# Attention and two expert layers on one core: the place of the turn of the maxima, of the last queries' transfers and of twelve remainders

## The chip, the cores and the metric

One core of one Trainium2 chip runs the whole program in one launch. The metric is the device time of that launch in microseconds (us), as the median of several runs. TensorE multiplies, VectorE, ScalarE and POOL (GpSimd) do the elementwise work, and SP issues nearly all DMAs; each of them works its own list of instructions strictly in order and waits for the others by semaphores.

## The reference

```python
# attention: batch 4, 8 heads, 576 positions, 64 per head
scores = (q @ k^T) / sqrt(64)
cum    = cumsum(log(clip(f, 1e-4, 1)))              # forget gates
scores = where(causal, -1e9, scores + cum[:, None] - cum[None, :])
scores = scores - max(scores)
attn   = exp(scores) / (sum(exp(scores)) + 1e-9)
x      = (attn @ v), heads side by side             # 2304 x 512
# first layer
h = ((x @ w1) * (x @ w2)) @ w3 ;  x = h @ w_out
# second layer: each row goes to the expert of its largest logit
e = argmax(x @ w_gate) ; out = gate(x) * sigmoid(x @ w_output_gate)[e] * (relu(x @ w1[e]) @ w2[e])
```

## The kernel before, in words

The attention runs over 16 pairs of heads (4 batches of 4 pairs). Each pair goes through the same stages, and pairs overlap: while one pair's probabilities are multiplied with its values, the next pair's scores are taken. The order of the work is written out by hand. `START` gives each stage of a pair a time in an imagined period of 9.8; `SHIFT` moves single stages of single pairs; all stages of all pairs are sorted by that time and issued in that order (L399 to L421), and every engine keeps that order. The numbers are places in a list, not times on the chip. `FILL` puts short products of zeros (L162) behind a stage, which only keep TensorE active.

The stages of pair n that matter here:

- `lk`, `lq`, `lv` load k, q and v (L188, SP). `kh`, `qh` round them to the short float format on ScalarE (L203), `kl`, `ql` take what is left over on VectorE (L210).
- `X1`, `X3`, `X2` are the scores by rows of queries (L217 by way of L219), each into a buffer of two PSUM banks; three such buffers go round. `m1`, `m3`, `m2`, `m0` take the row maxima on VectorE (L252).
- `qd` moves the last 64 queries of both heads into a block-diagonal tile `QD` by two DMAs (L205, L183). `XL` takes their scores (L244, L245), `mL` their maxima (L252).
- `Tm` turns the collected maxima by a product with the identity (L259), `tc` copies them out on ScalarE (L262), `mv` moves them by two DMAs into the row tile `MR` (L183).
- `GA` to `GD` are the scores once more, now by rows of keys and in full precision, and `HA` to `HD` add decay and maxima from `MR` to them in the same banks (L269); `eA` to `eD` take the exponentials on ScalarE (L289); `a0` to `a4` clear the part above the diagonal (L295) and `s1` to `s3` add the blocks up (L307), both on POOL.
- `p0`, `p1`, `p3` multiply the probabilities with the values (L316), `su` gives the sums (L332), both two pairs later in the list.
- For each batch, the sums are inverted: `rl` loads them, `rv` adds and takes reciprocals on VectorE (L356, L357), `rs` stores them (L359, SP). `xl` broadcasts the inverses for the first 512 rows (L74, SP) and `xm` multiplies them in on POOL (L367).
- `cr` clears, by one DMA of 771 KB in each of pairs 4 to 11, the rows `xs` into which the second layer's rows are scattered later (L377); the zeros are written on POOL (L375, L376).

Beside that, weights of the first layer are brought in as "pieces" of 512 KB each (class `Combined`, L424): step `c0` loads a piece (L462, SP), `c1` (ScalarE) to `c4` (VectorE) put its 64-bit numbers together as 32-bit ones (L469 to L475), `c5` rounds them on ScalarE (L478), and `c6` takes the remainder (L480), for the first 12 pieces on POOL, for all others on VectorE. One piece is done per pair. Behind the attention the pieces are multiplied, then both layers follow.

What stands in line in one period, before (phase in the period, from `START`):

```python
SP:      lq .3  ck 1.2  lk 2.6  zs 3.4  xl 4.2  rs 4.5  lv 5.7  c0 5.8  mv 6.6  rl 6.8  cr 7.6  qd 8.9
VectorE: kl 1.2  ql 1.3  c2 2.8  c3 3.4  c4 3.5  mL 3.5  m1 4.5  m3 7.3  m2 8.3  m0 8.6  rv 8.6
TensorE: GD, HD 1.5  XL 2.1  p0 3.3  Tm 3.6  X1 3.8  X3 4.7  X2 4.7  p1 5.1  p3 6.1  su 6.6  GA 8.4 ...
```

`X1`, `X3`, `X2` and `m1` to `m0` in this line belong to the next pair, `c3`, `c4` to an earlier piece.

Of the kernel before, what the change touches and what calls it, by code (L numbers as in the profile page):

```python
# [11 lines left out]
F32 = mybir.dt.float32  # L12
F32R = mybir.dt.float32r
# [15 lines left out]
P = 128  # L29
# [18 lines left out]

PERIOD = 9.8
START = {  # L50
# [8 lines left out]
}  # L59
SHIFT = {}  # L60

FILL = {(0, "X0"): 5, (0, "XL"): 10, (1, "X0"): 4, (1, "XL"): 4, (2, "X2"): 5, (2, "X0"): 5}

AFTER = {
    "K4_13": 4.4, "K4_14": 4.43, "K0_15": 15.6, "K0_16": 15.61, "K0_17": 15.62, "inputs": 11.36, "scores": 13.38,
# [11 lines left out]
def attention(nc, tc, ident, xT, rz, xs, wc, q, k, v, f):  # L77
# [7 lines left out]
    with (  # L85
# [16 lines left out]

        def decay_parts():
            SP.dma_start(out=fc, in_=f)
            V.tensor_scalar(out=fc, in0=fc, scalar1=1e-4, scalar2=1.0, op0=ALU.max, op1=ALU.min)
            A.activation(out=fc, in_=fc, func=ACTF.Ln)
            V.tensor_tensor_scan(c8, fc, fc, 0.0, ALU.add, ALU.bypass)
            V.tensor_scalar(out=EK[0:NH], in0=c8, scalar1=-8.0, scalar2=None, op0=ALU.mult)
            V.scalar_tensor_tensor(out=EK[NH:], in0=c8, scalar=-8.0, in1=EK[0:NH].bitcast(F32), op0=ALU.mult, op1=ALU.subtract)
# [15 lines left out]
        def rows(e, t):  # L125
            e.memset(t.bitcast(F32), 0.0)
            for h in range(2):
                e.memset(t[64 * h:64 * h + 3, :min(S, t.shape[1])].bitcast(F32), 1.0)

        def constants():  # L130
            rows(G, CKs[0])
            rows(V, OQ)
            for t in (OD, *QDs, *[t[:, S:] for x in KHs for t in x]):
                V.memset(t.bitcast(F32), 0.0)
            for h in range(2):
                V.memset(OD[64 * h:64 * h + 3, HALF[h]].bitcast(F32), 1.0)
                for t in (OQ, OD):
                    V.memset(t[64 * h:64 * h + 1].bitcast(F32), 0.0)
            V.memset(ones, 1.0)
            for t in Ms:  # L140
                V.memset(t, 0.0)
            G.memset(tri, 0.0)
            G.affine_select(
                out=tri[:, 512:640], in_=tri[:, 512:640], pattern=[[-1, P]],
                compare_op=ALU.is_ge, fill=NEG, base=0, channel_multiplier=1,
            )
            G.memset(tril, 0.0)
            for h in range(2):
                G.affine_select(
                    out=tril[64 * h:64 * h + 64, 512:S], in_=tril[64 * h:64 * h + 64, 512:S],  # L150
                    pattern=[[-1, SL]], compare_op=ALU.is_ge, fill=NEG, base=0, channel_multiplier=1,
                )
            for t in MRs + CKs[1:]:
                rows(G, t)
# [101 lines left out]
                )  # L256

        def turn(s):
            PE.matmul(s["x", 4][0:64, 896:1024], Ms[s["n"] % 2], ident, start=True, stop=True)  # L259

        def turned(s):
            A.activation(out=tl(s, "mt", (P,), F32R)[0:9], in_=s["x", 4][0:9, 896:1024], func=ACTF.Copy)  # L262

        def spread_maxima(s):
            t, MR = s["mt"], MRs[s["n"] % 2]
# [93 lines left out]
                    SP.dma_start(out=view(rz), in_=z)  # L359

        def first_tile(s, x):
            for i in {7: (0, 1), 11: (2, 3)}.get(s["n"], ()):
                d = tl(s, f"rb{i % 2}", (512,), bufs=1)
                if x == 0:
                    spread(nc, d, rz[i, :, 0:512])
                else:
                    G.tensor_tensor(out=xT[:, i, 0:512], in0=xT[:, i, 0:512], in1=d, op=ALU.mult)  # L367

        def clear_rows(s):

            e = s["n"] - 4
            if 0 <= e < E:
                if e == 0:
                    zt = st["zt"] = p3.tile([P, DM + 2], F32, name="zero", bufs=1)
                    G.memset(zt, 0.0)  # L375
                    G.memset(zt[:, DM + 1:], float(2 * N))  # L376
                SP.dma_start(out=xs[e * N:e * N + W].rearrange("(c p) d -> p c d", p=P), in_=st["zt"].unsqueeze(1).broadcast_to([P, W // P, DM + 2]))  # L377

        stages = {
# [44 lines left out]
class Combined:  # L424


    def __init__(self, nc, tc, xpool, raw, wo, w3t, last):
# [5 lines left out]
            self.pieces += [("o", j), (0, j), (1, j)]  # L433
            self.steps += [(0, j), (1, j)]
        self.at = {x: i for i, x in enumerate(self.pieces)}
        self.queue = [self.narrow(f"w{x}{j}", wo[j] if x == "o" else w3t[x, j], self.slot(i), None, nc.vector if i >= 12 else None) for i, (x, j) in enumerate(self.pieces)]
        self.done, self.acc, self.spare = [0] * 7, {}, None
        self.raw = [raw.tile([P, 8, 512], F32, name=f"raw{i}", tag="u") for i in range(2)]
        self.units = [None] * 3
# [853 lines left out]
```

## Time and profile before

| | |
|---|---|
| median of 3 runs | 795.99 us (795.97 to 798.34) |
| the profiled execution | 797.8 us, of it 796.2 us span from the first to the last instruction |
| TensorE busy | 772.3 us, 97% of the span |
| VectorE, ScalarE, POOL busy | 443.6, 276.3, 309.7 us |
| mean granted TensorE clock | 0.992 of full speed |

The profile lists, for one execution, the instructions of each engine with their start and length in us from the span's start. A line of the timeline gives start, length, engine, line of the kernel, operation, the tile written and the tiles read, their shapes, and in brackets how long the engine had idled before and what ended that. PEld is the loading of weights on TensorE, SPq the issuing of DMAs on SP: the length there is that of the issue, not of the transfer. A clock of 0.5 is 1.2 GHz, 1.0 is 2.4 GHz.

### The profile page before, as it was taken

The numbers are of one execution on the slowest core, as the hardware profiler recorded it, in microseconds if no ns is written. First come the engines' busy times: TensorE is split into PE (matmuls) and PEld (weight loads), VectorE is DVE, ScalarE is ACT, GpSimd is POOL, SyncE is SP. The second block draws the span as 40 slices with busy tenths as digits, with TensorE's granted clock in tenths as the row PEclk, the third lists the DMA queues.
The fourth block names the chain that finished last, engine by engine and source line by source line (L and its number), as shares of the span: only waits on it lengthen the run. The fifth ranks groups of instructions, "written<-read, shape, count | busy, mean of one in ns | idle before, by whom it ended". The sixth has DMA issues, their size and how long they took to land. (4 is left out here: it accounts for less than half of the span.)

```text
span 796.2 us, 13782 instructions
## 1 busy us (share of the span) xinstructions
PE 772.3 (97%) x5153; PEld 643.9 (81%) x5155; DVE 443.6 (56%) x986; ACT 276.3 (35%) x537; POOL 309.7 (39%) x343
## 2 busy tenths in 40 slices
PE   7999999899999999999999999999999999999995
PEld 4676776677888887887888788898797999999983
DVE  7687887887989723341341322346478735445620
ACT  2565666564566222212221221313321222322221
POOL 6577888994000210230230111033444444444520
PEclk9999999999999999999999999999999999999998
DMA  3556777425635110110100010053676556456460
GB/s 108 158 150 195 230 230 249 147 86 168 201 123 196 53 42 28 40 40 5 55 16 13 21 40 0 4 189 112 215 231 221 165 189 229 146 185 214 146 262 30
DMA packets 40212, 102.12 MB, mean 128 GB/s; under 512 B 8611, under 2 KB 9315, under 8 KB 39889
## 3 DMA queue, kind: packets, MB, share of 16 engines
q1 hardware_dynamic: 36960, 91.46, 35.9%
q0 software_dynamic: 3184, 9.77, 3.2%
q8 instruction: 41, 0.67, 0.4%
q14 instruction: 27, 0.21, 0.1%
HBM read 84.47 MB, written 16.51 MB: 127 GB/s over the span
## 5 line engine op out<-in xcount | busy, mean ns | idle before, releaser
L595 DVE TENSOR_TENSOR ga<-b,ga 128x512 f32<-128x512 f32 (+1 forms) x40 | 25.4, 636 | 144.0 <-PE b L567 143.2
L726 POOL DMA_INDIRECT xs<-xr,pos x18 | 19.5, 1084 | 173.5 <-DVE pos L720 126.6
L252 DVE CUSTOM_DVE_ANT_0 junk<-x,tri 128x256 f32<-128x256 f32 (+3 forms) x128 | 62.9, 491 | 24.3 <-PE x L217 16.5
L565 PE MATMUL h<-gh,ah 128*128 128x320 f32 (+4 forms) x224 | 67.2, 300 | 0.0
L566 PE MATMUL h<-gl,ah 128*128 128x320 f32 (+4 forms) x224 | 66.9, 299 | 0.0
L567 PE MATMUL h<-gh,al 128*128 128x320 f32 (+4 forms) x224 | 66.9, 299 | 0.0
L565 PE MATMUL b<-xh,w2h 128*128 128x512 f32 (+1 forms) x160 | 59.9, 375 | 0.0
L565 PE MATMUL a<-xh,w1h 128*128 128x512 f32 (+1 forms) x160 | 59.8, 374 | 0.0
L567 PE MATMUL a<-xh,w1l 128*128 128x512 f32 (+1 forms) x160 | 58.9, 368 | 0.0
L567 PE MATMUL b<-xh,w2l 128*128 128x512 f32 (+1 forms) x160 | 58.9, 368 | 0.0
L566 PE MATMUL a<-xl,w1h 128*128 128x512 f32 (+1 forms) x160 | 58.8, 368 | 0.0
L566 PE MATMUL b<-xl,w2h 128*128 128x512 f32 (+1 forms) x160 | 58.8, 368 | 0.0
L565 PE MATMUL y<-raw,gh 128*128 128x512 f32 x144 | 56.9, 395 | 0.0
L567 PE MATMUL y<-raw,gl 128*128 128x512 f32 x144 | 56.2, 390 | 0.0
L566 PE MATMUL y<-raw,gh 128*128 128x512 f32 x144 | 56.0, 389 | 0.0
L295 POOL TENSOR_SCALAR_AFFINE_SELECT PT<-PT 128x256 f32<-128x256 f32 (+1 forms) x80 | 42.3, 547 | 35.3 <-ACT PT L289 35.3
L597 ACT ACTIVATE gh<-ga 128x512 fp32r<-128x512 f32 (+1 forms) x40 | 23.6, 589 | 87.3 <-DVE ga L595 87.3
L558 POOL TENSOR_SCALAR bh<-rb 128x1024 fp32r<-128x1024 f32 x28 | 37.0, 1324 | 42.9 <-DMA rb<-e 41.0
L1019 DVE SCALAR_TENSOR_TENSOR hl<-h,hh 128x320 fp32r<-128x320 f32 (+4 forms) x56 | 25.3, 461 | 46.8 <-ACT hh L1018 46.6
L316 PE MATMUL v<-PT,vr 128*64 128x448 f32 (+4 forms) x384 | 50.8, 402 | 0.0
L581 POOL TENSOR_TENSOR xT<-xT,rz 128x512 f32<-128x512 f32 (+1 forms) x16 | 19.8, 1235 | 76.6 <-ACT w2h L478 76.5
L559 DVE TENSOR_TENSOR bl<-rb,bh 128x1024 fp32r<-128x1024 f32 x28 | 37.0, 1338 | 15.0 <-POOL bh L558 15.0
(613 smaller groups left out, 2116.2 us busy)
## 6 DMA issues: line engine op xcount, KB each, us to landing
ra<-e SPq DMA_DIRECT2D x28, 512.0 KB
rb<-e SPq DMA_DIRECT2D x28, 512.0 KB
w<-w3t SPq DMA_DIRECT2D x16, 512.0 KB
xs<-zero SPq DMA_DIRECT2D x8, 771.0 KB
vr<-v SPq DMA_DIRECT2D x16, 320.0 KB
kr<-k SPq DMA_DIRECT2D x16, 288.0 KB
qr<-q SPq DMA_DIRECT2D x16, 288.0 KB
wo<-wo SPq DMA_DIRECT2D x8, 512.0 KB
```

Of the source, the lines that this page charges most:

```text
L252: V.tensor_tensor_reduce(out=junk[:, :w], in0=s["x", i][:, 512 * h:512 * h + w] if i < 4 else s["x", i][:, 224:224 + S], in1=tri[:, 640 - ...
L295: G.affine_select(out=t, in_=t, pattern=[[0, 2], [1, w]], compare_op=ALU.is_ge, fill=0.0, base=0, channel_multiplier=-1,)
L316: PE.matmul(s["v"][HALF[h], 384 + q0:384 + q1], s["vr"][:, j, HALF[h]], place(s, j, h, q0, q1), start=(j == 0), stop=(j == 4 or q1 == P),)
L558: G.tensor_scalar(out=hi, in0=src, scalar1=1.0, scalar2=1.0, op0=ALU.mult, op1=ALU.mult)
L559: lo_eng.tensor_tensor(out=lo, in0=src, in1=hi.bitcast(F32), op=ALU.subtract)
L565: PE.matmul(ps, ah, bh, start=start and i == 0, stop=False)
L566: PE.matmul(ps, ah, bl, start=False, stop=False)
L567: PE.matmul(ps, al, bh, start=False, stop=stop and i == last)
L581: G.tensor_tensor(out=xv, in0=xv, in1=d, op=ALU.mult)
L595: V.tensor_tensor(out=ga[:, :w], in0=pb[:, :w], in1=ga[:, :w], op=ALU.mult)
L597: A.activation(out=gh[:, f, :w], in_=ga[:, :w], func=ACTF.Copy)
L1019: V.scalar_tensor_tensor(out=hl[:, f, :w], in0=ps[:, :w], scalar=0.0, in1=hh[:, f, :w].bitcast(F32), op0=ALU.max, op1=ALU.subtract)
```

## The change

The list is rearranged. The turn of a pair's maxima now stands behind the next pair's scores and writes into the free columns of the first of their buffers (not for the first and the last pair). The last queries' transfers come before the loads of values and piece and before the maxima's row, instead of behind the clearing. `c1` goes behind the copy of the turned maxima, `c6` one place before `mL`, and on VectorE for all pieces. The reciprocals `rv` go from behind `m0` to behind `mL`; the store `rs` stays where it is. The first 512 rows are multiplied one tile per pair (pairs 7, 8, 9, 10) instead of two in pair 7 and two in pair 11, and the zeros for the clearing are written in pair 2. In the first pair, `XL`, `mL` and what follows go ahead of the subtractions; some fills move. At the start, a part of the constants is written while the gates are loaded, and a one-column exponential behind the logarithm loads ScalarE's table early.

```diff
--- before.py
+++ after.py
@@ -48,18 +48,18 @@
 
 PERIOD = 9.8
 START = {
-    "lk": -16.99, "c0": -13.79, "c1": -10.39, "lq": -9.49, "ck": -8.57, "kh": -7.55, "c2": -7.02, "qh": -6.92,
-    "X1": -5.99, "m1": -5.27, "X3": -5.12, "X2": -5.07, "m3": -2.49, "X0": -1.58, "m2": -1.5, "m0": -1.24, "qd": -0.95,
-    "kl": 1.21, "XL": 2.1, "mL": 3.54, "Tm": 3.61, "tc": 3.98, "ql": 1.3, "mv": 6.59, "cr": 7.59, "GA": 8.35,
+    "lk": -16.99, "c0": -13.79, "c1": -4.9, "lq": -9.49, "ck": -8.57, "kh": -7.55, "c2": 2.78, "qh": -6.92,
+    "X1": -5.99, "m1": -5.27, "X3": -5.12, "X2": -5.07, "m3": -2.49, "X0": -1.58, "m2": -1.5, "m0": -1.24, "qd": -4.8,
+    "kl": 1.21, "XL": 2.1, "mL": 3.54, "Tm": 4.8, "tc": 4.85, "ql": 1.3, "mv": 6.59, "cr": 7.59, "GA": 8.35,
     "HA": 8.43, "GB": 8.46, "HB": 8.5, "GC": 8.77, "HC": 9.64, "eA": 10.17, "eB": 10.24, "eC": 11.25, "GD": 11.28,
     "HD": 11.31, "a0": 11.0, "a1": 11.6, "a4": 11.7, "c3": 13.19, "eD": 13.33, "c4": 13.3, "c5": 14.02, "lv": 15.51,
-    "s1": 13.9, "a2": 14.0, "a3": 14.1, "s2": 14.5, "c6": 17.0, "s3": 17.5, "p0": 22.91, "p1": 24.73,
-    "p3": 25.66, "su": 26.2, "xl": 33.6, "xa": 27.84, "sa": 28.24, "xm": 41.0, "zs": 32.77, "rl": 36.24, "rv": 57.6,
+    "s1": 13.9, "a2": 14.0, "a3": 14.1, "s2": 14.5, "c6": 23.12, "s3": 17.5, "p0": 22.91, "p1": 24.73,
+    "p3": 25.66, "su": 26.2, "xl": 33.6, "xa": 27.84, "sa": 28.24, "xm": 43.2, "zs": 32.77, "rl": 36.24, "rv": 62.36,
     "rs": 63.34,
 }
-SHIFT = {}
-
-FILL = {(0, "X0"): 5, (0, "XL"): 10, (1, "X0"): 4, (1, "XL"): 4, (2, "X2"): 5, (2, "X0"): 5}
+SHIFT = {(0, "XL"): -4.55, (0, "mL"): -5.9, (0, "Tm"): -1.8, (0, "tc"): -1.8, (0, "mv"): -3.49}
+
+FILL = {(0, "XL"): 10, (1, "X0"): 2, (0, "HA"): 3, (0, "HB"): 5, (1, "XL"): 4, (2, "X0"): 5, (1, "HA"): 2, (1, "HB"): 3}
 
 AFTER = {
     "K4_13": 4.4, "K4_14": 4.43, "K0_15": 15.6, "K0_16": 15.61, "K0_17": 15.62, "inputs": 11.36, "scores": 13.38,
@@ -102,8 +102,11 @@
 
         def decay_parts():
             SP.dma_start(out=fc, in_=f)
+            small_constants()
             V.tensor_scalar(out=fc, in0=fc, scalar1=1e-4, scalar2=1.0, op0=ALU.max, op1=ALU.min)
             A.activation(out=fc, in_=fc, func=ACTF.Ln)
+            A.activation(out=junk[:, 0:1], in_=Ms[0][:, 0:1], func=ACTF.Exp)
+            pads()
             V.tensor_tensor_scan(c8, fc, fc, 0.0, ALU.add, ALU.bypass)
             V.tensor_scalar(out=EK[0:NH], in0=c8, scalar1=-8.0, scalar2=None, op0=ALU.mult)
             V.scalar_tensor_tensor(out=EK[NH:], in0=c8, scalar=-8.0, in1=EK[0:NH].bitcast(F32), op0=ALU.mult, op1=ALU.subtract)
@@ -127,18 +130,24 @@
             for h in range(2):
                 e.memset(t[64 * h:64 * h + 3, :min(S, t.shape[1])].bitcast(F32), 1.0)
 
+        def small_constants():
+            rows(V, OQ)
+            for h in range(2):
+                V.memset(OQ[64 * h:64 * h + 1].bitcast(F32), 0.0)
+            for t in Ms:
+                V.memset(t, 0.0)
+
+        def pads():
+            for t in (*QDs, *[t[:, S:] for x in KHs for t in x]):
+                V.memset(t.bitcast(F32), 0.0)
+
         def constants():
             rows(G, CKs[0])
-            rows(V, OQ)
-            for t in (OD, *QDs, *[t[:, S:] for x in KHs for t in x]):
-                V.memset(t.bitcast(F32), 0.0)
+            V.memset(OD.bitcast(F32), 0.0)
             for h in range(2):
                 V.memset(OD[64 * h:64 * h + 3, HALF[h]].bitcast(F32), 1.0)
-                for t in (OQ, OD):
-                    V.memset(t[64 * h:64 * h + 1].bitcast(F32), 0.0)
+                V.memset(OD[64 * h:64 * h + 1].bitcast(F32), 0.0)
             V.memset(ones, 1.0)
-            for t in Ms:
-                V.memset(t, 0.0)
             G.memset(tri, 0.0)
             G.affine_select(
                 out=tri[:, 512:640], in_=tri[:, 512:640], pattern=[[-1, P]],
@@ -256,10 +265,12 @@
                 )
 
         def turn(s):
-            PE.matmul(s["x", 4][0:64, 896:1024], Ms[s["n"] % 2], ident, start=True, stop=True)
+            x = st[s["n"] + 1]["x", 1][:, 256:] if 0 < s["n"] < B * NP - 1 else s["x", 4][:, 896:]
+            s["t"] = x[0:64, :P]
+            PE.matmul(s["t"], Ms[s["n"] % 2], ident, start=True, stop=True)
 
         def turned(s):
-            A.activation(out=tl(s, "mt", (P,), F32R)[0:9], in_=s["x", 4][0:9, 896:1024], func=ACTF.Copy)
+            A.activation(out=tl(s, "mt", (P,), F32R)[0:9], in_=s["t"][0:9], func=ACTF.Copy)
 
         def spread_maxima(s):
             t, MR = s["mt"], MRs[s["n"] % 2]
@@ -359,7 +370,7 @@
                     SP.dma_start(out=view(rz), in_=z)
 
         def first_tile(s, x):
-            for i in {7: (0, 1), 11: (2, 3)}.get(s["n"], ()):
+            for i in {7: (0,), 8: (1,), 9: (2,), 10: (3,)}.get(s["n"], ()):
                 d = tl(s, f"rb{i % 2}", (512,), bufs=1)
                 if x == 0:
                     spread(nc, d, rz[i, :, 0:512])
@@ -369,11 +380,11 @@
         def clear_rows(s):
 
             e = s["n"] - 4
+            if e == -2:
+                zt = st["zt"] = p3.tile([P, DM + 2], F32, name="zero", bufs=1)
+                G.memset(zt, 0.0)
+                G.memset(zt[:, DM + 1:], float(2 * N))
             if 0 <= e < E:
-                if e == 0:
-                    zt = st["zt"] = p3.tile([P, DM + 2], F32, name="zero", bufs=1)
-                    G.memset(zt, 0.0)
-                    G.memset(zt[:, DM + 1:], float(2 * N))
                 SP.dma_start(out=xs[e * N:e * N + W].rearrange("(c p) d -> p c d", p=P), in_=st["zt"].unsqueeze(1).broadcast_to([P, W // P, DM + 2]))
 
         stages = {
@@ -433,7 +444,7 @@
             self.pieces += [("o", j), (0, j), (1, j)]
             self.steps += [(0, j), (1, j)]
         self.at = {x: i for i, x in enumerate(self.pieces)}
-        self.queue = [self.narrow(f"w{x}{j}", wo[j] if x == "o" else w3t[x, j], self.slot(i), None, nc.vector if i >= 12 else None) for i, (x, j) in enumerate(self.pieces)]
+        self.queue = [self.narrow(f"w{x}{j}", wo[j] if x == "o" else w3t[x, j], self.slot(i), None, nc.vector) for i, (x, j) in enumerate(self.pieces)]
         self.done, self.acc, self.spare = [0] * 7, {}, None
         self.raw = [raw.tile([P, 8, 512], F32, name=f"raw{i}", tag="u") for i in range(2)]
         self.units = [None] * 3
```

## Rows read from the trace of the kernel before

**Rows 1.** Windows: length; busy PE, PEld, DVE, ACT, POOL (instructions); clock, DMA share, GB/s.

```profile
10.00:190.00 180.00, 169.39 (x1802) 124.77 (x1801) 142.63 (x374) 101.36 (x171) 142.34 (x152) 0.98 0.57 178
190.00:510.00 320.00, 320.00 (x1482) 261.63 (x1481) 146.68 (x309) 99.05 (x189) 44.48 (x47) 1.00 0.18 58
```

**Rows 2.** Timeline of TensorE: the second turn and the last two.

```profile
28.00 0.43 PE L259 MATMUL xl<-ident,M 128*64 128x128 f32 x2
...
162.56 0.38 PE L259 MATMUL xl<-ident,M 128*64 128x128 f32 x2
...
172.19 0.27 PE L259 MATMUL xl<-ident,M 128*64 128x128 f32 x1
```

**Rows 3.** Timeline around the first clearing, and the window behind it.

```profile
62.83 0.41 SPq L377 DMA_DIRECT2D xs<-zero  x1
...
67.14 0.58 PE L244 MATMUL xl<-kh,QD 128*128 128x288 f32 x1 [1.90 <-DMA QD<-qh]
...
66.75:70.25 3.50, 3.11 (x12) 1.94 (x13) 0.77 (x2) 1.60 (x2) 2.34 (x3) 0.53 0.86 263
```

**Rows 4.** Timeline of the two pairs from 120 to 143 us.

```profile
120.14 0.43 PE L259 MATMUL xl<-ident,M 128*64 128x128 f32 x2
...
121.72 0.57 SPq L183 DMA_DIRECT2D MR<-mt  x1
...
126.29 0.40 PE L217 MATMUL gA<-MR,CK 64*128 64x288 f32 x2 [1.11 <-DMA MR<-mt]
...
129.91 2.53 POOL L367 TENSOR_TENSOR xT<-xT,rb 128x512 f32<-128x512 f32 x2
...
137.55 1.84 DVE L210 TENSOR_TENSOR ql<-qr,qh 128x576 fp32r<-128x576 f32 x1
...
142.89 0.43 PE L259 MATMUL xl<-ident,M 128*64 128x128 f32 x2 [1.93 <-DVE M L252]
```

**Rows 5.** Line 480, one remainder on POOL, one on VectorE: ns min/median/max, start.

```profile
L480 POOL TENSOR_TENSOR cw<-wo0u,cw x1: 1280/1280/1280, 51.0 to 51.0; 128x512 fp32r<-128x512 f32 x1
...
L480 DVE TENSOR_TENSOR gh<-wo4u,gh x1: 692/692/692, 190.7 to 190.7; 128x512 fp32r<-128x512 f32 x1
```

**Rows 6.** Timeline of an ordinary pair, from the queries' rounding to the row's use.

```profile
98.57 0.70 ACT L203 ACTIVATE qh<-qr 128x576 fp32r<-128x576 f32 x1
...
100.82 0.42 DVE L252 CUSTOM_DVE_ANT_0 junk<-x,tri 128x256 f32<-128x256 f32 x1 [0.99 <-PE x L217]
...
101.28 0.45 PE L217 MATMUL x<-CK,OQ 64*128 64x384 f32 x4
...
104.64 0.19 PEld L217 LDWEIGHTS gA<-MR,CK 64*128 64x128 f32 x2
```

**Rows 7.** Timeline of the start: first turn, third bank; and the window behind it.

```profile
16.44 0.43 PE L259 MATMUL xl<-ident,M 128*64 128x128 f32 x2 [1.79 <-DVE M L252]
...
22.30 0.60 PE L217 MATMUL gC<-qh,kh 64*128 64x448 f32 x4 [1.59 <-DVE M L252]
...
22.50:25.75 3.25, 3.25 (x26) 3.08 (x26) 1.67 (x3) 1.08 (x2) 0.06 (x1) 0.51 0.63 185
```

**Rows 8.** Timeline: a piece's issue and use, a row's issue and use.

```profile
15.45 0.42 SPq L462 DMA_DIRECT2D wo<-wo  x1
...
19.38 0.67 ACT L469 ACTIVATE wo0u<-wo 128x512 f32<-128x512 f32 x1 [2.20 <-DMA wo<-wo]
...
172.95 1.15 SPq L183 DMA_DIRECT2D MR<-mt  x2
...
175.45 0.29 PE L217 MATMUL gA<-MR,CK 64*128 64x288 f32 x2
```

**Rows 9.** Timeline: the reciprocals of a batch, and the store of one.

```profile
105.19 0.69 DVE L356 TENSOR_SCALAR z<-z 128x36 f32<-128x36 f32 x1
105.92 0.38 DVE L357 RECIPROCAL z<-z 128x36 f32<-128x36 f32 x1
...
151.00 0.65 SPq L359 DMA_DIRECT2D rz<-z  x1
```

## The prediction

> **What bounds the kernel now.** I read the windows first, then TensorE's timeline, then the queues. From 10 to 190 us, the attention, TensorE idles 10.6 us (180.00 - 169.39) at a mean granted clock of 0.98; in the 320 us behind it there is no idle time at all [rows 1]. So time won in attention arrives at the end undiminished, and it can only come from those 10.6 us and from the stretches at 1.2 GHz.
>
> The turn of the maxima (L259) marks a pair of heads. The last two stand 172.19 - 162.56 = 9.63 us apart with no wait on TensorE: that is its floor for a pair. From the second turn at 28.00 to the last at 172.19 there are 14 steps and 144.19 us, 9.4 more than 14 x 9.63 = 134.8 [rows 2]. I look for those 9.4, and for the start.
>
> **What is removed.**
> *Clearing.* In pair 4 SP's first clearing of `xs` leaves only at 62.83, because it waits for the memset of its zeros, which sits on POOL behind an addition and a remainder. The last queries' transfers are behind it on SP; TensorE idles 1.90 us for them at 67.14, and the clock then stands at 0.53 for the 3.5 us window: about 3.5 x 0.47 = 1.6 us more [rows 3]. The memset now runs two pairs earlier, with nobody on SP waiting (a short memset on POOL, whose slack hides it), and these transfers no longer stand behind a clearing. Gain 3.5; the lower bound is nothing, if another entry of SP's queue holds them.
>
> *First rows of the product.* From 120.14 to 142.89 two steps took 22.75, 3.5 over the floor. The four broadcasts of two tiles crowded the DMAs, so the maxima's row, issued at 121.72, kept TensorE waiting 1.11; then two multiplications on POOL (2.53 at 129.91) pushed its additions onto VectorE's subtractions (1.84 for one), and the turn waited 1.93 [rows 4]. Now one tile comes per pair, and POOL loses twelve remainders of 1.28 each [rows 5]. I take 3.0 of 3.5, since one multiplication still falls in each of four pairs; bounds 0 and 3.5.
>
> *The rest.* 9.4 - 3.5 - 3.5 = 2.4 us lie in small waits of the turn and in two pairs with reciprocals. Before the next scores, the turn waited for VectorE, and VectorE then idled 0.99 for the scores behind the turn [rows 6]. With the scores ahead, neither waits: 2.4, bounds 0 and 2.4.
>
> *Start.* TensorE waits 1.79 for the first turn and 1.59 before the third bank, and the clock is 0.51 for 3.25 us: 1.6 lost [rows 7]. The two subtractions leave the way to the first turn (nearest row 0.69 each [rows 5]), worth about 1.2; the fills moved behind the maxima's product keep TensorE active where it fell to 1.2 GHz, 1.6. In the second pair there is no probability product yet between turn and use of the row, so I give 1.0 back. Gain 1.8, bounds 0 and 3.4 (1.79 + 1.6). The early Exp table load and the split constants I cost at nothing: the warm-up matmuls cover them, and if that cover failed it would be one table load.
>
> **What is added.**
> *VectorE.* Twelve remainders at 0.69 [rows 5] stand ahead of the last queries' maxima. The cover is the 0.99 that VectorE now idles per pair [rows 6], so 0.3 remains: nothing. Upper bound 1.84 each, a subtraction of this kind when POOL is busy [rows 4]. On this pair of engines, the Trainium skill (SBUF — State Buffer, Who interferes with whom) says that a VectorE instruction with two SBUF inputs and a GpSimd instruction that reads SBUF block each other whole; by it a remainder could cost a whole POOL addition. That is the last rival below.
>
> *The row's way.* The last scores end at 101.28 + 0.45 = 101.73 with the turn (0.43 [rows 4]) ahead of them; with the turn behind, they end and it starts at 101.3. From the turn's start to the row's issue it is 172.95 - 172.19 = 0.76 [rows 2, 8], so the row leaves at about 102.1. Its first use loads weights at 104.64 [rows 6]: 2.55 us later. On an idle queue that does: in the last pair the row issued at 172.95 is in use at 175.45 without a wait [rows 8]. But the last queries' transfers now stand ahead of `v` and the piece, and SP must wait for `qh`, done at 98.57 + 0.70 = 99.27 [rows 6]. Two issues like the row's (1.15) and one of `v`, taken as long as a piece's (0.42) [rows 8]: the piece leaves at about 100.9, just ahead of the row. A piece took 19.38 - 15.45 = 3.93 us to its use behind another load [rows 8], here to 104.8; a row behind it is late by about 0.15. Ten loaded pairs: +1.5. Bounds: 0 (the row overtakes) and 2.0 each, as the crowded row took 126.29 - 121.72 = 4.57 [rows 4]. The idle-queue row alone would put this term at 0. The Trainium skill (DMA: Bandwidth & Descriptors, Queues, rings and completion order) says that each DMA engine takes descriptors in ring order; by that the row does wait for the load before it, which is the side I took.
>
> *The reciprocals.* They move from behind the scores' maxima to just behind the last queries' maxima, and their store on SP (`rs`) keeps its place, now ahead of the last queries' transfers. Before, SP found them done. Now, in the frame of rows 6, that maximum ends at about 99.8 (0.99 before 100.82), the reciprocals last 106.30 - 105.19 = 1.1 [rows 9], so the store leaves at 100.9 and takes 0.65 [rows 9], the queries' two 1.15, `v` 0.42: the piece at 103.2, the row at 103.6. Queued behind the waiting store are all of these, and TensorE waits for the row. It lands at 103.6 + 2.5 = 106.1 on an idle queue, 103.2 + 3.93 = 107.1 with the piece; used at 104.64. So 1.5 to 2.5 late; I take 2.4, as the piece is always there. It happens in two pairs (the third store comes after the last pair): +4.8.
>
> **Sum.** -3.5 - 3.0 - 2.4 - 1.8 + 1.5 + 4.8 = -4.4. The profiled execution took 797.8 around its span of 796.2, 1.8 above the median of the runs, 795.99; the difference taken off the median gives 791.6.
>
> **Rivals.**
> 1. *The store doesn't bite* and the row keeps up: VectorE runs ahead in those pairs, or the small row overtakes. For it: even in the crowded pair the row was only 1.11 late [rows 4]. Against: SP works strictly in order. 791.6 - 4.8 - 1.5 = 785.3.
> 2. *The clock falls after both stores.* TensorE idles 2.4 us there; 1.90 and 1.59 were followed by 1.2 GHz [rows 3, 7], 1.93 at 142.89 was not. Each fall costs 1.6: 794.8.
> 3. *Slower: the row is late in every loaded pair.* Place: the maxima's product of the first bank, on the DMAs behind `v`, the piece and the clearing. With 1.0 us in ten pairs for 0.15: +8.5, 800.1. It decides from (4.4 + 1.5) / 10 = 0.6 us per pair on. For it: 4.57 in the crowded pair; against: that pair also had four broadcasts.
> 4. *VectorE becomes the bound*: remainders of 1.84, 0.85 over the cover, twelve times: +10.2, 801.8. Against: POOL has 1.28 less to do per pair, right where the subtractions were slowed.
>
> **Numbers.** Forecast 0.36, rival 1 0.27, rival 2 0.22, rival 3 0.10, rival 4 0.05. This kernel can tell about 0.3% (2.4 us) from no change: faster is below 793.6, slower above 798.4. The forecast's own range is 788.5 to 794.5. Faster: most of the forecast (0.33), rival 1 (0.27), a third of rival 2 (0.07): 0.67. Slower: rivals 3 and 4 less a part that ends within: 0.12. Same: 0.21. The range leaves out what is slowest: 784.5 to 797.5.
>
> **What would show it.** Right: no wait for the last queries' transfers at the fifth pair and no clock below 1 there; turns mostly 9.6 to 9.9 apart; in two pairs a wait of TensorE for the row (L183) of about 2.4 us, with the reciprocals' store on SP directly before the queries' transfers; idle time of VectorE before the next scores' maxima gone; the first turn near 15.2. Wrong: waits for the row in every pair (rival 3), TensorE waiting for maxima in most pairs (rival 4), or no wait at all in the reciprocals' pairs (rival 1).

## The result, and the profile after

The changed kernel takes 808.07 us (median of 4 runs, 807.56 to 808.88) against 796.05 for the kernel before beside it: ratio 1.0145, 95% interval 1.0124 to 1.0165, so 11.5 us slower. The forecast was 791.6, with a range of 784.5 to 797.5: wrong in sign and outside its range. The profiled execution has a span of 805.9 us, 9.7 more than before.

The windows of the changed kernel, with the columns of [rows 1]:

```profile
10.00:190.00 180.00, 166.09 (x1717) 125.31 (x1715) 137.65 (x378) 100.13 (x164) 112.07 (x135) 0.97 0.53 168
10.00:15.00 5.00, 4.25 (x22) 2.51 (x19) 4.17 (x15) 1.37 (x2) 3.55 (x6) 0.66 0.35 98
66.75:70.25 3.50, 3.46 (x31) 2.17 (x32) 2.41 (x8) 2.48 (x4) 3.50 (x5) 1.00 0.16 53
90.00:95.00 5.00, 3.75 (x25) 2.76 (x27) 3.13 (x11) 2.94 (x5) 3.80 (x5) 0.80 0.40 120
165.00:170.00 5.00, 3.31 (x34) 3.21 (x36) 2.05 (x4) 1.89 (x3) 0.41 (x1) 0.81 0.34 115
170.00:175.00 5.00, 4.96 (x44) 3.57 (x44) 1.82 (x7) 3.01 (x5) 4.61 (x6) 0.85 0.12 20
190.00:510.00 320.00, 320.00 (x1501) 259.74 (x1498) 150.80 (x315) 99.05 (x187) 49.86 (x53) 1.00 0.20 64
```

TensorE now idles 13.9 us of the attention's 180 instead of 10.6. At the fifth pair, where [rows 3] had a clock of 0.53, it is 1.00. The clock falls in three other places: ahead of the first turn, between 10 and 15 us, where it stood at 1.00 before; near 93; and near 168 us. Each fall costs about 1.7 us, as (1 - 0.66) x 5 for the first. The 320 us behind the attention are full, as before. So the loss lies in the attention.

The timeline of the changed kernel at some of the turns (now L270):

```profile
28.48 0.43 PE L270 MATMUL x<-ident,M 128*64 128x128 f32 x2
...
39.95 0.32 PE L270 MATMUL x<-ident,M 128*64 128x128 f32 x1
...
49.97 0.13 PEld L270 LDWEIGHTS x<-ident,M 128*64 128x64 f32 x1 [0.17 <-DVE M L261]
49.97 0.32 PE L270 MATMUL x<-ident,M 128*64 128x128 f32 x1
...
53.40 0.18 PEld L226 LDWEIGHTS gA<-MR,CK 64*128 64x128 f32 x2 [0.19 <-DMA MR<-mt]
...
128.34 0.32 PE L270 MATMUL x<-ident,M 128*64 128x128 f32 x1
...
174.72 0.32 PE L270 MATMUL x<-ident,M 128*64 128x128 f32 x1
182.80 0.27 PE L270 MATMUL xl<-ident,M 128*64 128x128 f32 x1
```

From 28.48 to the last at 182.80 are 14 steps as in [rows 2], 154.32 us, 10.1 more than there. A plain one (39.95 to 49.97) takes 10.02, where the floor of [rows 2] is 9.63: the loading of the weights waits 0.19 for the row, and 0.17 for a maximum at the turn. Most of the rest lies in three stretches: the four steps from 70.07 to 115.48 (pairs 6 to 9), of 11.2 to 11.7 each, and the two pairs with reciprocals, 12.86 (115.48 to 128.34) and 14.95 (159.77 to 174.72). The first step, 28.48 to 39.95, takes 11.47; it belongs to the start.

The first reciprocals' pair, SP's queue and TensorE:

```profile
112.40 1.86 DVE L367 TENSOR_SCALAR z<-z 128x36 f32<-128x36 f32 x1
114.30 0.38 DVE L368 RECIPROCAL z<-z 128x36 f32<-128x36 f32 x1
114.70 0.63 SPq L370 DMA_DIRECT2D rz<-z  x1
115.44 0.52 SPq L192 DMA_DIRECT2D QD<-qh  x1
...
115.48 0.32 PE L270 MATMUL x<-ident,M 128*64 128x128 f32 x1 [1.04 <-DVE M L261]
...
116.69 0.54 SPq L197 DMA_DIRECT2D vr<-v  x1
117.29 0.42 SPq L473 DMA_DIRECT2D w<-w3t  x1
117.80 1.20 SPq L192 DMA_DIRECT2D MR<-mt  x2
...
120.91 0.40 PE L226 MATMUL gA<-MR,CK 64*128 64x288 f32 x2 [1.95 <-DMA MR<-mt]
```

And the second:

```profile
158.99 0.67 SPq L370 DMA_DIRECT2D rz<-z  x1
...
159.77 0.32 PE L270 MATMUL x<-ident,M 128*64 128x128 f32 x1 [0.77 <-DVE M L261]
...
162.72 1.21 SPq L192 DMA_DIRECT2D MR<-mt  x2
...
166.69 0.40 PE L226 MATMUL gA<-MR,CK 64*128 64x288 f32 x2 [3.45 <-DMA MR<-mt]
```

Store, queries' transfers, `v`, piece and row stand in the order that the forecast gave, and TensorE waits for the row: 1.95 and 3.45. The turn, too, waits 1.04 and 0.77 for maxima that now stand behind the reciprocals on VectorE; the first of these waits makes the step to 115.48 long. Behind the second wait for the row the clock stands at 0.81 and 0.85 for 10 us, worth (0.19 + 0.15) x 5 = 1.7.

Pairs 6 to 8 show something the forecast did not have. First the kernel before, SP's queue behind a row, then the changed one:

```profile
80.71 1.14 SPq L183 DMA_DIRECT2D MR<-mt  x2
...
82.63 0.46 SPq L377 DMA_DIRECT2D xs<-zero  x1
83.13 1.92 SPq L183 DMA_DIRECT2D QD<-qh  x2
...
85.10 0.59 SPq L188 DMA_DIRECT2D qr<-q  x1
...
89.02 0.68 ACT L203 ACTIVATE qh<-qr 128x576 fp32r<-128x576 f32 x1 [0.48 <-DMA qr<-q]
...
90.49 0.39 PE L217 MATMUL x<-kh,qh 64*128 64x256 f32 x2
```

```profile
82.05 1.18 SPq L192 DMA_DIRECT2D MR<-mt  x2
...
84.01 0.45 SPq L388 DMA_DIRECT2D xs<-zero  x1
84.52 1.98 SPq L197 DMA_DIRECT2D qr<-q  x1
...
90.10 0.68 ACT L212 ACTIVATE qh<-qr 128x576 fp32r<-128x576 f32 x1 [1.81 <-DMA qr<-q]
...
90.83 0.39 PE L226 MATMUL x<-kh,qh 64*128 64x256 f32 x2 [1.25 <-ACT qh L212]
```

Behind the clearing stood the transfers of the last queries; now the load of the *next pair's* queries stands there. In this pair its issue is held for 1.98, the data land 5.6 behind its start (90.10 - 84.52), where they took 3.9 before (89.02 - 85.10), and the scores wait 1.25 for them; the clock then stands at 0.80 and 0.86 from 90 to 100, another 1.7. At 79 and 126 us the scores wait 0.44 and 0.31 for rounded queries.

### The profile page after: what moved, and what is told of

Its sections match the earlier page's. It is cut to its first block, busy times and chain, and to the rows that moved or that the text cites. A ratio compares the mean times of both kernels' runs of the same rounds, so it can differ in the third digit from the quotient of the medians.

```text
span 805.9 us, 13785 instructions
## 1 busy us (share of the span) xinstructions
PE 778.5 (97%) x5156; PEld 650.7 (81%) x5156; DVE 443.5 (55%) x998; ACT 279.4 (35%) x538; POOL 285.1 (35%) x331
## 5 line engine op out<-in xcount | busy, mean ns | idle before, releaser
L261 DVE CUSTOM_DVE_ANT_0 junk<-x,tri 128x256 f32<-128x256 f32 (+3 forms) x128 | 62.8, 490 | 22.0 <-PE x L226 13.6
L306 POOL TENSOR_SCALAR_AFFINE_SELECT PT<-PT 128x256 f32<-128x256 f32 (+1 forms) x80 | 34.7, 454 | 66.5 <-ACT PT L300 64.2
L327 PE MATMUL v<-PT,vr 128*64 128x448 f32 (+4 forms) x384 | 54.1, 404 | 0.0
L570 DVE TENSOR_TENSOR bl<-rb,bh 128x1024 fp32r<-128x1024 f32 x28 | 36.4, 1315 | 15.3 <-POOL bh L569 15.3
```

Source lines behind the costliest of these rows:

```text
L261: V.tensor_tensor_reduce(out=junk[:, :w], in0=s["x", i][:, 512 * h:512 * h + w] if i < 4 else s["x", i][:, 224:224 + S], in1=tri[:, 640 - ...
L306: G.affine_select(out=t, in_=t, pattern=[[0, 2], [1, w]], compare_op=ALU.is_ge, fill=0.0, base=0, channel_multiplier=-1,)
L327: PE.matmul(s["v"][HALF[h], 384 + q0:384 + q1], s["vr"][:, j, HALF[h]], place(s, j, h, q0, q1), start=(j == 0), stop=(j == 4 or q1 == P),)
L570: lo_eng.tensor_tensor(out=lo, in0=src, in1=hi.bitcast(F32), op=ALU.subtract)
```

## The experiments

The kernel before ran beside each of them, with medians from 796.05 to 798.78, so the ratios are compared and not the medians; "us" in the table is (ratio - 1) x 796. By the medians alone three of the differences from the change that follow come out smaller: 10.9 for recip_back, 4.9 for clear_later and 9.1 for store_later, instead of 12.3, 6.9 and 10.3. The edits are to the changed kernel unless said otherwise, and show only the entries that differ.

| kernel | median us | ratio (95%) | against before, us |
|---|---|---|---|
| the change | 808.07 | 1.0145 (1.0124 to 1.0165) | +11.5 |
| recip_back | 797.21 | 0.9991 (0.9973 to 1.0009) | -0.7 |
| clear_later | 803.15 | 1.0058 (1.0034 to 1.0082) | +4.6 |
| row_first | 810.54 | 1.0181 (1.0112 to 1.0250) | +14.4 |
| turn_back | 813.73 | 1.0190 (1.0148 to 1.0232) | +15.1 |
| recip_clear | 794.53 | 0.9953 (0.9936 to 0.9969) | -3.7 |
| recip_qd | 801.92 | 1.0038 (1.0021 to 1.0056) | +3.0 |
| recip_clear_pool | 795.19 | 0.9959 (0.9947 to 0.9972) | -3.3 |
| zeros_early | 794.26 | 0.9948 (0.9931 to 0.9964) | -4.1 |
| zeros_tiles | 792.78 | 0.9932 (0.9909 to 0.9954) | -5.4 |
| zeros_tiles_rem | 793.81 | 0.9942 (0.9921 to 0.9964) | -4.6 |
| start_added | 795.26 | 0.9963 (0.9949 to 0.9977) | -2.9 |
| start_clear | 794.84 | 0.9961 (0.9943 to 0.9979) | -3.1 |
| store_later | 798.99 | 1.0016 (0.9997 to 1.0035) | +1.3 |
| store_clear | 795.95 | 0.9971 (0.9954 to 0.9987) | -2.3 |

### One part of the change undone

**recip_back**: the reciprocals go back behind the next scores' maxima.

```diff
-"rv": 62.36
+"rv": 57.6
```

> The change with one number taken back: the reciprocals stand behind the scores' maxima again, so SP finds them done. Theory (SP's queue: the store waits for the reciprocals, and the row of maxima, values and piece wait behind the store): the two waits of TensorE for the row in the reciprocals' pairs (1.95 and 3.45 us) and the clock's fall behind the second (about 1.7) go, about 7 us less than the change's 808.1: 801. Rival (VectorE's load is the loss, wherever its work stands): within 1 us of 808.1.

One due time is worth 12.3 us (1.0145 - 0.9991), more than the theory's 7, and with it the kernel stands level with the one before.

**clear_later**: the clearing goes behind the next queries' load.

```diff
-"cr": 7.59
+"cr": 11.2
```

> The change with the clearing issued behind the next queries' load instead of ahead of it. Theory (SP's queue: the later turn lets the row, and with it the clearing and the next queries' load behind it, leave later, so the rounded queries are late for the scores, which now stand ahead of the turn): the waits of the scores for the rounded queries in pairs 6 to 10 go, with the clock's fall in pair 8: about 4 us less than 808.1, 804. Rival (VectorE's load): within 1 us of 808.1, since nothing on VectorE changes.

6.9 us (1.0145 - 1.0058), more than the 4 expected, and the rival is out. The turns of pairs 4 to 8 are 9.75 to 10.05 apart, and behind 30 us no scores wait for rounded queries; the reciprocals' pairs still take 11.99 and 14.84.

**row_first**: the row goes ahead of `v` and the piece.

```diff
-"lv": 15.51, "c0": -13.79
+"lv": 16.45, "c0": -13.1
```

> The change with the loads of values and piece issued behind the row of maxima instead of ahead of it. Theory (the row waits for transfers issued just ahead of it): the 0.2 us per loaded pair, the 1.1 us of pair 1 and part of the waits in the reciprocals' pairs go: about 4 us less than 808.1, 804. Rival (the row is late only because the turn is later): less than 1 us.

A miss: no gain. Its timeline:

```profile
81.57 1.17 SPq L192 DMA_DIRECT2D MR<-mt  x2
82.83 0.34 SPq L197 DMA_DIRECT2D vr<-v  x1
...
84.46 1.97 SPq L197 DMA_DIRECT2D qr<-q  x1
...
90.36 0.39 PE L226 MATMUL x<-kh,qh 64*128 64x256 f32 x2 [1.36 <-ACT qh L212]
```

In plain pairs the row comes to its product in time (two steps of 9.71 between the turns at 38.29 and 57.71), but `v` now stands between row and load too, and the scores wait for queries in seven pairs, 0.6 to 1.5 each. What one stage wins on this queue, the next one pays.

**turn_back**: the turn ahead of the next scores again, in its own buffer.

```diff
-"Tm": 4.8, "tc": 4.85
+"Tm": 3.61, "tc": 3.98
-x = st[s["n"] + 1]["x", 1][:, 256:] if 0 < s["n"] < B * NP - 1 else s["x", 4][:, 896:]
+x = s["x", 4][:, 896:]
```

> The change with the turn alone put back ahead of the next scores, into the last queries' own buffer; everything else as changed. Theory (the turn's place starts both chains on SP): the row leaves 1.45 us earlier, the rounded queries are needed 0.4 us later, about 5 us less than 808.1: 803, with the waits behind the reciprocals' store left. Rival (the turn's move is a gain, as the prediction had it, and the loss comes from the other parts): 808 to 812.

A miss too. (The edit also moves the first pair's turn ahead.) The row does not leave earlier against the scores, since the queries' transfers, `v` and the piece are still ahead of it on SP; it is late by 0.7 to 1.4 in several pairs, and by 3.29 and 3.43 in the two with the store. With the early queries' transfers and the early store, the turn's place is not what costs.

### Two causes, or one

**recip_clear**: `rv` and `cr` both back.

> The changed kernel with two due times put back: the reciprocals behind the next scores' maxima (rv 57.6) and the clearing behind the queries' load (cr 11.2). Theory (two separate losses on SP's queue: the store that waits for the reciprocals, worth 808.1 - 797.2 = 10.9, and the queries' load behind row and clearing, worth 808.1 - 803.2 = 4.9, which add): 808.1 - 10.9 - 4.9 = 792.3, no wait of the scores for rounded queries left, steps of 9.7 to 10.1 in pairs 4 to 9. Rival (one loss that either edit relieves, an overfull SP queue): about 797, no better than the reciprocals alone.

0.9953 of 796.05 is 792.3: the theory's number, but in part by luck, since the theory added differences of medians. By the ratios the two edits alone give 12.3 and 6.9, and together 15.3 (1.0145 - 0.9953): two losses, but they overlap by some 4 us. From 80 to 120 us TensorE is without a gap but for 0.04, and the step from 90.43 to 100.39 is 9.96. What is left is elsewhere; the worst place of its timeline:

```profile
148.80 1.74 POOL L378 TENSOR_TENSOR xT<-xT,rb 128x512 f32<-128x512 f32 x1
...
149.32 1.77 DVE L491 TENSOR_TENSOR raw<-w11u,raw 128x512 fp32r<-128x512 f32 x1
...
151.02 0.75 DVE L261 CUSTOM_DVE_ANT_0 junk<-xl,tril 128x576 f32<-128x576 f32 x1
...
151.83 0.51 PE L226 MATMUL x<-kh,qh 64*128 64x384 f32 x4 [1.47 <-DVE M L261]
```

A remainder on VectorE that starts during POOL's multiplication takes 1.77; the others of this kind take 0.68 to 0.89 in this trace. The rest of the multiplication (150.54 - 149.32 = 1.22) and 0.69 make 1.91. The maxima behind it come late and TensorE waits 1.47. This happened in one of the four pairs with a multiplication. The Trainium skill (SBUF — State Buffer, Who interferes with whom) says that an instruction of VectorE with two SBUF inputs contends with one of GpSimd that reads SBUF, and that this contention is an exclusive lock; this row agrees with it, nearly to the sum.

**store_later**: only the store moves, behind the row; VectorE's order is the changed kernel's.

```diff
-"rs": 63.34
+"rs": 66.0
```

> The changed kernel with the reciprocals' store moved behind the maxima's row on SP (rs 66.0); VectorE's order, the reciprocals' early place among it, is the changed kernel's. Theory (the store is the cause: it keeps SP waiting with the row behind it): the waits for the row of 1.95 and 3.45 in the two pairs fall to the 0.6 to 1.2 of other pairs, and the time to between 797 and 800, near the kernel with the reciprocals put back (0.9991). Rival (the reciprocals on VectorE ahead of the next scores' maxima are the cause, by the turn's waits of 1.04 and 0.77): 806 to 808, no better than the change (1.0145).

10.3 us back (1.0145 - 1.0016), as the theory had it: 1.0016 of 796.05 is 797.3. The first reciprocals' pair:

```profile
112.72 0.38 DVE L368 RECIPROCAL z<-z 128x36 f32<-128x36 f32 x1
...
113.91 0.32 PE L270 MATMUL x<-ident,M 128*64 128x128 f32 x1 [1.03 <-DVE M L261]
...
114.72 1.17 SPq L192 DMA_DIRECT2D MR<-mt  x2
116.00 0.62 SPq L370 DMA_DIRECT2D rz<-z  x1
...
117.22 0.29 PE L226 MATMUL gA<-MR,CK 64*128 64x288 f32 x2
```

The row leaves 0.8 behind the turn instead of 2.3 (117.80 - 115.48), and no wait is left at its product, nor in the second such pair, whose step is 10.03. The turn still waits 1.03 for the maxima that stand behind the reciprocals: that is what their place on VectorE costs, 2.0 us in all by recip_back (1.0016 - 0.9991), which the intervals allow to be nothing.

**store_clear**: the same with `"cr": 11.2`.

> The same with the clearing behind the queries' load as well (cr 11.2). Theory (store and clearing are the two causes, both on SP): like the kernel with reciprocals and clearing put back, 0.9953, so 792 to 794. Rival (VectorE's order): 0.7 to 1.0 per pair for the turn in two pairs, and up to 1.0058, the kernel with the clearing alone put back: 797 to 801.

0.9971 (793.7) lies within the theory's 792 to 794, 1.4 us above recip_clear with overlapping intervals: the store and the clearing are the main causes, and VectorE's order is small. It is not free: in the traced execution, the slowest of twelve, the turn waits 1.21 and 1.69 for maxima that stand behind the reciprocals.

**recip_qd**: recip_back with the last queries' transfers behind row and clearing, as before.

```diff
-"qd": -4.8
+"qd": -0.95
```

> The changed kernel with the reciprocals put back (rv 57.6) and the last queries' transfers back behind row and clearing (qd -0.95). Theory (the row, 1.2 us later than before, is late at its product by 0.2 to 1.2 us a pair because the queries' transfers, v and the piece are ahead of it; without those two issues of 0.58 each it is in time, and the queries' load also leaves earlier relative to them): 797.2 - 3 = about 794, waits for the row in ordinary pairs below 0.1. Rival (the queries' transfers ahead of the row cost nothing; behind row and clearing they are late at the last scores): 797 to 801, waits of the last scores for their queries.

The rival was right: 3.7 us slower than recip_back. With the turn behind the next scores the row and the clearing come later, and behind them these transfers come too late:

```profile
87.74 0.37 PE L253 MATMUL xl<-kh,QD 128*128 128x288 f32 x1 [1.68 <-DMA QD<-qh]
```

### The forecast's gains, added one by one

**zeros_early**: the kernel before, with the memset of the zeros two pairs earlier and nothing else.

```diff
+            if e == -2:
+                zt = st["zt"] = p3.tile([P, DM + 2], F32, name="zero", bufs=1)
+                G.memset(zt, 0.0)
+                G.memset(zt[:, DM + 1:], float(2 * N))
             if 0 <= e < E:
-                if e == 0:
-                    zt = st["zt"] = p3.tile([P, DM + 2], F32, name="zero", bufs=1)
-                    G.memset(zt, 0.0)
-                    G.memset(zt[:, DM + 1:], float(2 * N))
```

> The kernel before with one edit: the memset of the zeros two pairs earlier. Theory (the forecast's clearing term is right: 1.90 of waiting and 1.6 of slow clock at the fifth pair go): 796.0 - 3.5 = 792.5, no wait of 1.90 at 67 us, clock 1.0 there. Rival (the wait moves to another entry of SP's queue, or is given back in the next pairs): 795 to 796.

4.1 us, near the forecast's 3.5, from moving two memsets. In its trace the last scores of that pair wait for nothing, and the clock from 60 to 70 us is 1.00.

**zeros_tiles**: with the product's first tiles one per pair as well.

```diff
-for i in {7: (0, 1), 11: (2, 3)}.get(s["n"], ()):
+for i in {7: (0,), 8: (1,), 9: (2,), 10: (3,)}.get(s["n"], ()):
-"xm": 41.0
+"xm": 43.2
```

> The kernel before with the early zeros and with the product's first tiles one per pair. Theory (the forecast's term of the first rows is right: four broadcasts and two multiplications at once cost 3.5, one per pair 0.5): 0.9948 x 796.0 - 3.0 = 788.9, no wait of 1.33 for the row at 123 us and of 1.94 for the turn at 140. Rival (each of four pairs now pays a part: a broadcast late in one, POOL's multiplication beside VectorE's subtractions in the other): 791 to 793, small waits in four pairs.

1.3 us by the medians of the ratios, within the intervals of nothing. The steps of the scores from 127.5 on are 11.13, 10.70 and 10.41: three of the four pairs pay a part, as the rival had it.

**zeros_tiles_rem**: and the first twelve remainders on VectorE.

```diff
-nc.vector if i >= 12 else None
+nc.vector
-"c6": 17.0
+"c6": 23.12
```

> The same with the first twelve remainders on VectorE as well. Theory (VectorE has room for 0.69 a pair here too, and POOL's additions come earlier): within 1 us of the kernel without it. Rival (here, with the turn ahead of the next scores and VectorE's maxima on the way to it, a remainder ahead of the last queries' maxima delays the turn by 0.3 to 0.7 a pair): slower by 3 to 8, waits of the turn for the maxima in most pairs.

The same within the measurement (+0.8), but the mechanism of the rival is there: pairs 5 to 12 take 10.13 to 10.17 with few exceptions, where zeros_tiles mostly has 9.8 to 10.1, and the turn waits:

```profile
64.41 0.89 DVE L480 TENSOR_TENSOR cw<-w00u,cw 128x512 fp32r<-128x512 f32 x1
65.23 0.75 DVE L252 CUSTOM_DVE_ANT_0 junk<-xl,tril 128x576 f32<-128x576 f32 x1
...
66.03 0.43 PE L259 MATMUL xl<-ident,M 128*64 128x128 f32 x2 [0.26 <-DVE M L252]
```

**recip_clear_pool** asks the same with the turn behind the scores: recip_clear with these remainders on POOL.

```diff
-"c6": 23.12
+"c6": 17.0
-nc.vector)
+nc.vector if i >= 12 else None)
```

> The kernel with reciprocals and clearing put back, and the first twelve pieces' remainders back on POOL behind its additions (c6 17.0). Theory (VectorE has room, so its twelve remainders of 0.69 cost nothing; POOL had room too except behind the product's first tiles): within 2 us of the kernel with the two due times put back. Rival (a remainder on VectorE delays the maxima and with them the turn, by 0.3 to 0.7 us in twelve pairs): faster than that kernel by 4 to 8 us. Other side: if POOL's remainders delay its additions, slower by 1.28 in the four pairs with multiplications, about 5.

0.9959 against 0.9953: there the remainders cost nothing on either engine.

**start_added**: zeros_tiles_rem with the new start (the change with turn, queries' transfers and reciprocals put back; the first pair's turn keeps its early place). It also takes over the change's places of `c1` and `c2`, which no run moves alone.

> The changed kernel with the turn, the last queries' transfers and the reciprocals all put back: zeros, tiles, remainders and the new start are left. Theory (what lost is only the turn and what follows it on SP; the forecast's start term of 1.8 is right): 1.8 below the kernel with zeros, tiles and remainders, so about 787 if that one stands at 789. Rival (the start's gain is lost by the third pair, as in the changed kernel, where a lead of 2.2 at the second pair's last scores was a lag of 0.7 one pair later): equal to the kernel without it.

1.7 us slower than zeros_tiles_rem with overlapping intervals: no gain. The first turn is early, but TensorE waits before it and behind it, as its timeline and a window show, and in this execution the clock falls all the same:

```profile
15.29 0.43 PE L270 MATMUL xl<-ident,M 128*64 128x128 f32 x2 [1.62 <-DVE M L261]
...
16.59 0.58 PE L226 MATMUL x<-kh,qh 64*128 64x256 f32 x2 [0.87 <-ACT qh L212]
```

```profile
17.50:20.00 2.50, 2.50 (x16) 1.45 (x14) 2.21 (x8) 0.00 (x0) 0.00 (x0) 0.57 0.51 160
```

In the trace of the next kernel, with the same start and waits of 1.63 and 0.90, it does not fall:

```profile
17.50:20.00 2.50, 2.50 (x23) 1.37 (x19) 2.14 (x9) 0.51 (x1) 0.00 (x0) 1.00 0.58 166
```

**start_clear**: start_added with `"cr": 11.2`.

> The kernel with zeros, tiles, remainders and start, and the clearing moved behind the next queries' load (cr 11.2), so that the last queries' transfers come ahead of it. Theory (a clearing of 1.0 to 1.5 us of SP's time ahead of the last queries' transfers delays the last scores by 0.3 to 0.5 in some pairs): 1 to 3 us faster than the kernel with the clearing in its old place. Rival (the transfers are in time either way): the same within 0.5.

The same (0.9961): with the old turn, row and clearing leave early enough that it hardly matters who stands behind the clearing. The trace of before has one such wait, 0.53 of the last scores at 88.46.

Eight kernels beat both, with intervals below 1: the six of this part, recip_clear and store_clear. zeros_tiles has the lowest ratio, but zeros_early, zeros_tiles_rem and recip_clear, among others, cannot be told from it.

## Why the prediction was wrong

Two steps failed and turned the sign. The term of the reciprocals, +4.8, was mis-sized: 12.3 was measured. And the load of the next queries behind the clearing had no term: it cost 3.0 to 6.9. Two of the gains, first rows and start, 4.8 together, hardly came.

The ladder zeros_early, zeros_tiles, zeros_tiles_rem, start_added, start_clear, recip_clear, recip_back, change carries every term, each a difference of ratios x 796 and uncertain by some 2 us.

- **Clearing (-3.5): right.** -4.1, and in the changed kernel no wait and a clock of 1.00 at 67 us.
- **First rows (-3.0): too much.** -1.3 by the ratios; in the traces the five steps from the turn at 117 us on take 51.83 instead of 52.25. The waits of 1.11 and 1.93 in [rows 4] became four smaller ones, 0.28, 0.35, 0.87 and 0.23 in zeros_tiles. The step that failed is "I take 3.0 of 3.5": a broadcast and a multiplication spread out are not hidden by being spread.
- **Start (-1.8): not there.** +1.7 in start_added, which cannot be told from nothing. In the changed kernel itself the early part came true: first turn at 15.82 (forecast near 15.2), no fall of the clock behind it, the second pair's last scores 2.1 earlier than before (24.23 against 26.35). But a fall came ahead of the turn, with a clock of 0.66 from 10 to 15 us, at a wait of 0.76 for the last queries' transfers that ended at 11.52; the forecast did not have it. By the third pair's, they were 0.7 later than before (36.6 against 35.9), through a wait for the row of 1.09, about the 1.0 that the forecast gave back, and 0.8 at the scores. A lead in the first pair is worth nothing unless the second pair can keep it.
- **VectorE (nothing): right**, by recip_clear_pool, and rival 4 is out. In the changed kernel VectorE is busy for 443.5 us, as before, and waits for scores ahead of its maxima, 13.6 us in all by the page against 16.5 before.
- **The rest and the row's way (-2.4 + 1.5 = -0.9): the sum was right**, -0.6 from start_clear to recip_clear, where neither the clearing nor the store is in the way; with its uncertainty it cannot be told from nothing either. The parts behaved as follows: the row is 0.19 late in a plain pair, for 0.15; but the turn did not cease to wait. It now lies in a buffer of the next scores, behind the first half of their maxima, and waits 0.17 for these in a plain pair. I had said "neither waits" and not asked what the turn's new place waits for.
- **The reciprocals (+4.8): the mechanism right, the size far off.** 12.3, of which the store's place is 10.3 (store_later); the other 2.0 is within the uncertainty and fits the turn's waits for maxima behind the reciprocals (1.04 and 0.77 in the change, 1.03 and 0.38 in store_later), which the term did not have. The waits for the row were well sized: 1.95 + 3.45 = 5.4 against 4.8. One reading under them was not: the forecast has the reciprocals last 1.1 by [rows 9], but in the first pair they take 2.28 (112.40 to 114.68). The addition in front takes 1.86 there and ends with an addition on POOL that began at 112.11 and took 2.11; in the third batch, with POOL idle, it takes 0.17. What the term left out is mostly the clock. Its mean over the launch was 0.987 to 0.991 in the change's four runs, and 0.994 to 0.998 in eleven of store_later's twelve (0.990 in the other). An estimate from the means, 0.9890 and 0.9954, is 0.0064 x 800 = 5.1 us. The traces of the two, whose spans differ by 8.0, show where. The two pairs' steps are 12.86 + 14.95 = 27.8 against 11.14 + 10.03 = 21.2, so 6.6 of it is there: the waits, and 1.7 for the clock behind the second, which was rival 2 for one of the two stores. Another 1.6 lies ahead of the first store, where the clock of the change fell near 93 us behind a wait of 1.25 for queries; store_later waits 0.49 at that place and its clock stays at 1.00. Nothing of the edit lies before that place, so this fall is not shown to be the store's, and its cause stays open. The 10.3 of the ratios is more than the 8.0 of the traces because the two traced executions lie 0.5 on either side of their medians, and because the kernel before was slower beside store_later (797.55) than beside the change (796.05).
- **Not in the sum: the next queries' load.** 3.0 with the reciprocals back (0.9991 - 0.9953), 6.9 with them early (1.0145 - 1.0058). This is the failed step that decided the sign together with the store. The forecast moved the row 1.45 later (102.1 against 100.64 in the trace of before) and priced only the row's user. But SP works in order, and behind the row stand the clearing and the load of the next queries. In the trace of before the clearing left 2.3 behind the start of the pair's scores (82.63 - 80.31); in the changed kernel 4.9 (84.01 - 79.15). The load itself left 4.8 behind it before (85.10 - 80.31) and 5.4 now, only 0.6 later; but now the clearing stands directly ahead of it, and its data took 5.6 instead of 3.9. In recip_clear the load leaves 4.3 behind them (83.33 - 79.03), with the clearing behind it, and no scores wait. The forecast also took the last queries' transfers from behind the clearing and did not ask what would stand there instead.

Added up: -4.1 - 1.3 + 0.8 + 1.7 - 0.2 - 0.6 + 3.0 + 12.3 = +11.6, with -0.2 from start_added to start_clear and the +0.8 of the remainders. That it meets the +11.5 measured is no evidence: differences along a ladder add up to its end, and in another order the load has 6.9 and the reciprocals 8.4 (1.0058 - 0.9953).

Both rivals that were slower than before, 800.1 and 801.8, stay below the 808.07. Rival 4, the higher one, is out; rival 3 had the right sign and the wrong place: the row is not 1.0 late in every loaded pair, it is 0.2 late in most and 2 to 3.5 in two. Of the traces' signs, "two pairs with a wait for the row of about 2.4" and "the store directly before the queries' transfers" came true; "turns mostly 9.6 to 9.9 apart" and "idle time of VectorE before the next scores' maxima gone" did not.

## What to carry to other kernels

When a step moves later on an in-order queue, price everything behind it on that queue, not only its own user: here the row's delay passed through the clearing to the next pair's loads. A store that waits for a compute engine belongs behind the transfers that someone is waiting for; moving that one entry was worth 10 us of the 12 here. And where a big transfer is taken out from ahead of one load, look which load now stands behind it.

## What was not expected of the hardware

An issue on SP right behind the 771 KB clearing can be held: the queries' load for 1.98 us at one of the changed kernel's eight clearings, for 0.47 to 0.67 at the others; the trace does not show what sets it apart. And a wait of 1.25 us on TensorE in the changed kernel was followed by a clock of 0.80 and 0.86 over 10 us, while the 1.95 at 120.91 was followed by a clock of 1.00; the same start with nearly the same waits was followed by a clock of 0.57 in start_added and of 1.00 in start_clear. The length of one wait alone does not tell whether the clock falls.
